# Seven instead of five layer-1 weight blocks resident beside a recurrent scan

## The chip, the cores and the metric

One core of one Trainium2 chip runs the whole program. The metric is the device time of one execution in microseconds (us); less is better. Engines are named as in the profile: PE (TensorE matmuls), PEld (its weight loads), DVE (VectorE), ACT (ScalarE), POOL (GpSimd) and SP (SyncE, which issues all DMAs here).

## The reference

A recurrence over 768 time steps (4 batches, 8 heads, head size 40, a 40x40 state each) gives a tensor that is read as 3072 tokens of 320 features. Two gated feed-forward layers follow, both 320 to 1536 to 320:

```python
for t in range(S):
    y[:, :, t] = einsum('bhd,bhde->bhe', r[t], state)
    Sa = einsum('bhde,bhe->bhd', state, a[t])
    state = state * w[t] - einsum('bhd,bhe->bhde', Sa, b[t]) + einsum('bhd,bhe->bhde', v[t], k[t])
x = y.transpose(0, 2, 1, 3).reshape(3072, 320)
x = (silu(x @ w_gate) * (x @ w_val)) @ w_out        # layer 1
x = (sigmoid(x @ w_gate2) * (x @ w_val2)) @ w_out2  # layer 2
```

## The kernel before, in words

**The recurrence.** `attention` cuts the 768 steps into 12 chunks of 64 and turns each chunk into matmuls. For chunk m, `prep_a` forms the products of keys and queries (`kps`, L364, in four groups, with ACT L372 and DVE L374 behind each), and leaves a matrix `bn`. `prep_b` sends a part of `bn` through DRAM (L393 and L400) and then solves a triangular system on DVE: L409, L410 and 15 pairs of L417 (multiply) and L423 (reduce), each pair longer than the last. In this text that is **the solve** of chunk m, and a **step** is the time from one solve's L409 to the next one's. `chain` carries the state through the chunk (L506, L524, L535), and `post` forms the chunk's output `ysb` (L570 to L607).

**The feed-forward.** The tokens come in 12 blocks of 256 (one for each chunk), and each layer's weights in 12 blocks of 128 hidden features. One token block with one weight block is a **unit**: `gate` (16 matmuls of 128x256, L809; ACT L813 and L817; DVE L815 and L816; POOL L818) and `add` (6 matmuls of 128x320, L827). Each layer has 144 units. Weights come as float64 bit patterns, and `load_w` turns them into a high and a low part. It does a block in three **pieces**, each with one DMA (L699), five DVE instructions (L707, L711, L712, L716, L717), one on ACT (L727) and three or four on POOL (L708, L729 to L735).

**What runs beside what.** While the recurrence runs, layer-1 units run between its matmuls. This is `extra(m, ys)`: it splits chunk m's output into high and low parts (`split`, L755 to L771; **the split** in this text), stores the split block to DRAM (`xd`), and runs a unit with each weight block that is in SBUF by then. The number is kept in `used`. Five blocks are loaded early: three into a pool `wa` before the first chunk's units, two into `wt` and `wq`, which hold decay powers before that. Seven more (`more`) go into tiles of the recurrence as these come free, from chunk 10 on. After the recurrence, `stream` runs the units that are left of layer 1 (`w1[used[blk]:]`, with `load_x`, `each1` and `end1`) and then all of layer 2. `load_w2` converts the 12 weight blocks of layer 2 beside the rest of layer 1, one piece in each of three units of a token block.

**What sets the order.** `merge` (L624) interleaves the generators of an iteration m: `cp(m)`, `prep_b(m + 1)`, `prep_a(m + 2)`, `ahead(m)` (which holds `extra(m - 1)`) and `more`. Each stream has a pair (width of a step, offset), such as `NX = (0.1658, 0.2)` for `ahead`, and the least offset plus steps times width goes next. A scheduler then orders each engine's instructions. The engines run them strictly in that order.

Of the kernel before, what the change touches and what calls it, by code (L numbers as in the profile page):

```python
# [18 lines left out]
P = 128  # L19
# [1 line left out]
W = 16  # L21
C = 64
NS = 16
NFA = 5
NWB = 2
DM = H * D
PW = 64 + D
DFF = 1536
# [11 lines left out]
F_HIGH = (1.875 - 2.0**-23) * 2.0**16  # L40


def attention(ctx, tc, st, ident, ins, banks, extra, more):

# [507 lines left out]
    def post(m):  # L554
# [4 lines left out]
        for bp in range(2):  # L559
# [26 lines left out]
            for part in range(2):  # L586
                for h in range(H):
                    hp, h2 = divmod(h, 2)
                    for b2 in range(2):
# [11 lines left out]
                            stop=part == 1 and h == H - 1,  # L601
                            tile_position=(0, 64 * b2),
                        )
            ysb = wk.tile([P, DM + 64], F32, tag="ysb", name="ysb", bufs=3)
            yf, pf = yps.rearrange("p h d -> p (h d)"), pn[:, DM * bp : DM * bp + DM]
            nc.vector.tensor_tensor(out=ysb[:, 0:DM], in0=yf, in1=pf, op=ALU.mult)
            nc.vector.tensor_tensor(out=ysb[:, DM:], in0=yf[:, 256:DM], in1=pf[:, 256:DM], op=ALU.mult)  # L607
# [54 lines left out]
    for m in range(-1, NCH + 1):  # L662
        todo = []
        if 0 <= m < NCH:
            todo.append((cp(m), *NP))
        if 0 <= m < NCH - 1:
            todo.append((prep_b(m + 1), *(NB if m else QC)))
        if 2 <= m + 2 < NCH:
            todo.append((prep_a(m + 2), *(NA if m else QD)))
        todo.append((ahead(m), *(NX if m > 0 else QX)))  # L670
        if more is not None:

            free = {NCH - 2: [f"lq{NCH % 3}", f"tkb{NCH % 3}"]}
            free[NCH - 1] = [f"lq{(NCH + 1) % 3}", f"tkb{(NCH + 1) % 3}", "part0"]
            free[NCH] = ["part1", f"lq{(NCH + 2) % 3}", "part3", f"tkb{(NCH + 2) % 3}", "ut", "rbd", "part2"]
            todo.append((more(free.get(m, []), (raw_of(wk, ("sn", "zt", "x1t")), (pmm, "mm")) if m >= NCH - 1 else None), *NM))
        merge(todo)
# [308 lines left out]
def rwkv_moe_kernel(ctx, tc, r, k, v, w, a, b, aw0, aw, aa, akb, av, avt, art, w1a, w2a, out):  # L986
# [11 lines left out]
    with ExitStack() as c1:  # L998
# [1 line left out]
        x_p, h_p = pool("m_x", 1), pool("m_h", 2)  # L1000
        wa, st = pool("m_wa", NFA - 2), pool("at_static", 1)
        w1, w2, tags, spare_tags, used = [], [], [], [], []
        first = [(wa, "w8")] * (NFA - 2) + [(st, "wt"), (st, "wq")]

        with ExitStack() as c2:
            pool2 = lambda n, b: c2.enter_context(tc.tile_pool(name=n, bufs=b, space=PSUM))
            ffn = None

            def banks():

                nonlocal ffn
                ptp, pzy, pqu, pg, pmm, po = (pool2(f"a_{n}", 1 + (n == "tp")) for n in ("tp", "zy", "qu", "pg", "mm", "po"))
                ffn = Ffn(nc, ident, ([raw_of(st)], x_p, h_p, ptp, [(pg, "gv")], po), True)
                return ptp, pzy, pqu, pmm, po

            def more(new, spare):
                if spare is not None and len(ffn.raw) == 1:
                    ffn.raw.append(spare[0])
                    ffn.pg.append(spare[1])
                n = NF - len(w1)  # L1020
                spare_tags.extend(new[n:])
                for tag in new[:n]:
                    tags.append(tag)
                    yield from ffn.load_w(st, tag, layers[0], len(w1))
                    w1.append(ffn.w)

            def extra(m, ys):
                if m >= 0:
                    used.append(len(w1))
                    x = ffn.split(ys.pop(m))  # L1030
                    nc.sync.dma_start(out=xd[m], in_=x.bitcast(F32))
                    yield
                    yield from ffn.ffn(x, w1[: used[m]], True, "po")
                    for u in range(2):
                        ob = h_p.tile([P, DM], F32, tag="ob", name="ob", bufs=1)
                        nc.scalar.copy(out=ob, in_=ffn.o[u])
                        nc.sync.dma_start(out=xs[1][2 * m + u], in_=ob)
                        yield
                for f in {-2: range(NFA - 2), 1: range(NFA - 2, NFA)}.get(m, ()):
                    yield from ffn.load_w(*first[f], layers[0], f)  # L1040
                    w1.append(ffn.w)

            attention(c2, tc, st, ident, (aw0, aw, aa, akb, av, avt, art), banks, extra, more)

        with ExitStack() as c2:
            pool2 = lambda n, b, **kw: c2.enter_context(tc.tile_pool(name=n, bufs=b, **kw))
# [14 lines left out]

            ahead = load_w2()

            def load_x(blk):
                ffn.x = (x_q, x_p)[blk % 2]
                x = ffn.new_x()
                nc.sync.dma_start(out=x.bitcast(F32), in_=xd[blk])
                yield x

            def split_x(blk):  # L1070
                xin = y_p.tile([P, 2, DM + 64], F32, tag="xin", name="xin")
                src = xs[1][2 * blk : 2 * blk + 2].rearrange("u p e -> p u e")
                nc.sync.dma_start(out=xin[:, :, 0:DM], in_=src)
                nc.sync.dma_start(out=xin[:, :, DM:], in_=src[:, :, 256:DM])
                yield
                ffn.x = (x_q, x_p)[blk % 2]
                yield from ffn.split_steps([xin[:, 0], xin[:, 1]])

            parts = {}
# [1 line left out]
            def each1(blk, f):  # L1081
# [2 lines left out]
                    nc.sync.dma_start(out=part, in_=xs[1][2 * blk : 2 * blk + 2].rearrange("u p e -> p u e"))  # L1084
                if 1 <= f <= 3:
                    next(ahead, None)
                if blk == NB - 1 and f == NF - 1 - used[blk]:
                    for _ in ahead:
                        pass

# [38 lines left out]
                flag.append(fl)  # L1129

            flag, jobs, seen = [], [], []
            for blk in range(NB):
                jobs.append((w1[used[blk] :], True, "po", load_x(blk), partial(each1, blk), partial(end1, blk)))
            for blk in range(NB):
                jobs.append((w2, False, "po", split_x(blk), partial(check, blk), partial(end2, blk)))
# [54 lines left out]
```

## Time and profile before

| | |
|---|---|
| three runs, us | 1457.96, 1460.96, 1463.65 (median 1460.96) |
| the profiled execution, span, us | 1462.6 |
| PE, DVE, POOL, ACT busy, us | 1282.7, 858.1, 678.0, 535.1 |
| mean granted TensorE clock | 0.890 |

The span runs from the first instruction to the last of the one profiled execution; no other time is listed for that execution, and its span lies 1.6 us above the median of the runs. A busy PE is not a PE at its peak, since the ends of matmuls are modelled and overlap. The granted clock is given as a share of full speed: 1.0 is 2.4 GHz and 0.5 is 1.2 GHz. The profile counts an fp32 matmul of the recurrence twice (two passes), so four `kps` matmuls of the program are eight in a row of the trace.

### The profile page before, as it was taken

Reading aid. Unit: us, or ns where it says so; the run is one execution under the profiler, and the core shown is the slowest. Engines: PE = TensorE matmul, PEld = TensorE weight load, DVE = VectorE, ACT = ScalarE, POOL = GpSimd, SP = SyncE. Lnnn points to the kernel's source line nnn. Section 1 sums busy time; section 2 is a strip of 40 time slices with the busy share of each in tenths; the row PEclk is TensorE's granted clock in tenths of the full one; section 3 lists DMA queues with packets and bytes.
Section 4 is the critical chain, followed back from the end, with each engine's and each line's share of the span. In section 5 each row is a group of like instructions: output and inputs, shape, how many; then the busy total and the mean of one; then the engine's idle time right before and its main releaser. Section 6 shows DMA issues by size and latency. Waiting matters only on the chain.

```text
span 1462.6 us, 32637 instructions
## 1 busy us (share of the span) xinstructions
PE 1282.7 (88%) x13197; PEld 1207.8 (83%) x13197; DVE 858.1 (59%) x1644; ACT 535.1 (37%) x1260; POOL 678.0 (46%) x800
## 2 busy tenths in 40 slices
PE   4548867789899899887979999999999999999996
PEld 4447756678888888786979988889999999999996
DVE  8679759388756865876687999886311122112111
ACT  5223524253445444533433332333333333333331
POOL 4378468352213222245587888996222222222221
PEclk7556858696989999886999999999999999999998
DMA  5854884946355446425234654442100000100000
GB/s 139 206 114 107 170 195 94 187 97 159 88 125 140 102 119 147 93 62 132 87 99 155 185 164 132 140 135 95 63 21 21 21 21 22 30 21 21 12 13 17
DMA packets 242096, 144.49 MB, mean 99 GB/s; under 512 B 186768, under 2 KB 218512, under 8 KB 241552
## 3 DMA queue, kind: packets, MB, share of 16 engines
q1 hardware_dynamic: 241936, 142.31, 37.6%
q8 instruction: 106, 1.74, 0.5%
q14 instruction: 54, 0.44, 0.1%
HBM read 104.00 MB, written 38.27 MB: 97 GB/s over the span
## 4 chain that ended last, share of the span: by engine, by line
PE 43%; DVE 30%; DMA 10%; POOL 5%; SPq 5%; issue 5%; ACT 1%; POOLq 0%; DVEq 0%; ACTq 0%
PE g L809 21%; PE po L827 11%; DVE pr L417 7%; PE gv L809 4%; DVE part L423 4%; DMA sn<-nd 3%; DVE dt L712 3%; DVE dt L711 2%; POOL dt L708 2%; SPq L219 2%; DVE ds L717 2%; DMA raw<-in_w_dram 2%; DVE g L815 1%; PE kps L364 1%; DVE dt L707 1%
## 5 line engine op out<-in xcount | busy, mean ns | idle before, releaser
L809 PE MATMUL g<-x,w 128*128 128x256 f32 x3552 | 495.3, 284 | 12.8 <-DVE g L815 11.8
L809 PEld LDWEIGHTS g<-x,w 128*128 128x128 f32 x3552 | 462.8, 190 | 19.0 <-DVE g L815 16.7
L818 POOL TENSOR_TENSOR hl<-g,hh 128x256 fp32r<-128x256 f32 x288 | 220.5, 768 | 452.8 <-ACT hh L817 409.5
L816 DVE TENSOR_TENSOR g<-g,g 128x256 f32<-128x256 f32 x222 | 93.7, 422 | 307.7 <-PE g L809 297.7
L827 PE MATMUL po<-w,hh 128*128 128x320 f32 x1152 | 230.0, 314 | 2.8 <-ACT hh L817 1.4
L817 ACT CAST hh<-g 128x256 fp32r<-128x256 f32 x288 | 117.0, 406 | 302.8 <-DVE g L816 276.4
L809 PE MATMUL gv<-x,w 128*128 128x256 f32 x1056 | 173.4, 318 | 30.4 <-DVE g L816 18.2
L809 PEld LDWEIGHTS gv<-x,w 128*128 128x128 f32 x1056 | 152.9, 217 | 38.2 <-DVE g L816 24.2
L827 PEld LDWEIGHTS po<-w,hh 128*128 128x128 f32 x1152 | 179.0, 191 | 4.6 <-ACT hh L817 2.6
L417 DVE TENSOR_TENSOR pr<-part,sn 128x4 f32<-128x4 f32 (+4 forms) x180 | 150.1, 834 | 4.0
L827 PE MATMUL po<-w,hl 128*128 128x320 f32 x576 | 145.1, 318 | 2.9 <-POOL hl L818 2.9
L813 ACT ACTIVATE g<-g 128x256 f32<-128x256 f32 x222 | 85.1, 384 | 142.5 <-PE g L809 109.4
L708 POOL TENSOR_SCALAR dt<-dt 128x384 f32<-128x384 f32 (+1 forms) x72 | 109.2, 1519 | 40.9 <-DVE dt L707 38.0
L729 POOL TENSOR_TENSOR dt<-dt,w 128x384 f32<-128x384 f32 (+1 forms) x72 | 79.3, 1101 | 78.4 <-ACT w L727 32.3
L827 PEld LDWEIGHTS po<-w,hl 128*128 128x128 f32 x576 | 93.8, 191 | 5.2 <-POOL hl L818 4.2
L423 DVE TENSOR_REDUCE part<-pr 128x2 f32<-128x4 f32 (+4 forms) x180 | 88.9, 494 | 4.0
L364 PE MATMUL kps<-lq,kbt 104*128 104x128 f32 x384 | 69.4, 338 | 18.6 <-DVE lq L374 15.6
L364 PEld LDWEIGHTS kps<-lq,kbt 104*128 104x128 f32 x384 | 61.8, 244 | 23.2 <-issue 13.2
L727 ACT CAST w<-dt 128x384 fp32r<-128x384 f32 (+1 forms) x72 | 35.6, 495 | 98.6 <-DVE dt L712 91.5
L570 PE MATMUL aps<-rbd,ut 104*128 104x128 f32 x384 | 61.5, 307 | 9.3 <-DVE ysb L607 3.0
L707 DVE TENSOR_SCALAR dt<-raw 128x384 int32<-128x384 int32 (+1 forms) x72 | 44.9, 624 | 40.2 <-DMA raw<-in_w_dram 34.1
L372 ACT ACTIVATE bn<-kps 64x256 f32<-64x256 f32 x96 | 36.4, 379 | 84.5 <-PE kps L364 46.6
(129 smaller groups left out, 1762.1 us busy)
## 6 DMA issues: line engine op xcount, KB each, us to landing
raw<-in_w_dram SPq DMA_DIRECT2D x48, 384.0 KB
xd<-x SPq DMA_DIRECT2D x12, 896.0 KB
x<-xd SPq DMA_DIRECT2D x12, 896.0 KB
raw<-in_w_dram SPq DMA_DIRECT2D x24, 320.0 KB
pn<-pd SPq DMA_DIRECT2D x46, 160.0 KB
ld<-in_a_kb_dram SPq DMA_DIRECT2D x22, 320.0 KB
ld<-rd SPq DMA_DIRECT2D x44, 160.0 KB
sn<-nd SPq DMA_DIRECT2D x24, 256.0 KB
```

The costliest lines, as they stand in the source:

```text
L364: nc.tensor.matmul(kps[:, n].rearrange("p h t -> p (h t)"), lhsT=kbt[0:PW, n, :], rhs=lq[m % 3][0:PW, 4 * g4 + n].rearrange("p h t -> p (h ...
L417: nc.vector.tensor_tensor(out=o, in0=xs[:, 0:kk, None, 0:n].to_broadcast([P, kk, 2, n]), in1=sn[:, None, 0:n, n : n + 2].rearrange("p o s ...
L423: nc.vector.tensor_reduce(out=xs[:, 0:kk, n : n + 2], in_=o, axis=AX.X, op=ALU.add)
L570: nc.tensor.matmul(aps[:, n, h2], lhsT=ut[0:PW, x, 2 * h2 : 2 * h2 + 2].rearrange("p u s -> p (u s)"), rhs=rbd[0:PW, x, h2].rearrange("p b ...
L708: nc.gpsimd.tensor_scalar(out=t.bitcast(F32), in0=t.bitcast(F32), scalar1=F_LOW, scalar2=F_HIGH, op0=ALU.max, op1=ALU.min)
L729: sub(out=tf, in0=tf, in1=w.bitcast(F32), op=ALU.subtract)
L809: nc.tensor.matmul(gv[n], lhsT=p, rhs=q, start=e == 0, stop=e == len(seq) - 1)
L813: nc.scalar.activation(out=g, in_=gv[0], func=AF.Sigmoid)
L816: nc.vector.tensor_tensor(out=g, in0=gv[1], in1=g, op=ALU.mult)
L817: nc.scalar.copy(out=hh, in_=g)
L818: self.heng.tensor_tensor(out=hl, in0=g, in1=hh.bitcast(F32), op=ALU.subtract)
L827: self.nc.tensor.matmul(ops[u], lhsT=p[:, us], rhs=q, start=first and n == 0, stop=last and n == 2)
```

## The change

The tables that set sizes and pools:

```diff
-NFA = 5
-NWB = 2
+NFA = 7
+NWB = 1
@@ post
-            ysb = wk.tile([P, DM + 64], F32, tag="ysb", name="ysb", bufs=3)
+            ysb = wk.tile([P, DM + 64], F32, tag="ysb", name="ysb", bufs=2)
@@ merge loop of attention
-        todo.append((ahead(m), *(NX if m > 0 else QX)))
+        todo.append((ahead(m), *((1.33 / (6 + units(m - 1)), NX[1]) if m > 0 else QX)))
@@ rwkv_moe_kernel
-        first = [(wa, "w8")] * (NFA - 2) + [(st, "wt"), (st, "wq")]
+        first = [(wa, "w8")] * 3 + [(st, "wt"), (st, "wq")] + [(wa, "w8")] * (NFA - 5)
@@ extra
-                for f in {-2: range(NFA - 2), 1: range(NFA - 2, NFA)}.get(m, ()):
+                for f in {-2: range(3), 1: range(3, 5), 2: range(5, 6), 3: range(6, NFA)}.get(m, ()):
                     yield from ffn.load_w(*first[f], layers[0], f)
@@ call of attention: units is
+ lambda m: min(len(w1), NFA) + (3 if m == 1 else 0)
@@ kernel
-    nc = _bacc.Bacc("TRN2", target_bir_lowering=False, num_devices=1)
+    nc = _bacc.Bacc("TRN2", target_bir_lowering=False, num_devices=1, dynamic_dma_scratch_size=512)
```

The pool `wa` has five tiles instead of three. Weight blocks 5 and 6 are loaded behind the units of token blocks 2 and 3, before iterations in which no weights were loaded; so `more` has two blocks less to load for layer 1, and layer 2 finds two more tiles free. The space comes from the scratch for dynamic transfers, one of three `ysb` buffers and one of two `wb` buffers. The width of `ahead`'s step now follows the number of units. The numbers in `used` go from 3, 3, 5, 5, 5, 5, 5, 5, 5, 6, 8, 11 to 3, 3, 5, 6, 7, 7, 7, 7, 7, 8, 10, 12, so 82 units of layer 1 instead of 66 run beside the recurrence, and 62 instead of 78 behind it. The last token block has all 12 units there and gets no job in `stream`:

```diff
-            for blk in range(NB):
+            left = [blk for blk in range(NB) if used[blk] < NF]
+            for blk in left:
                 jobs.append((w1[used[blk] :], True, "po", load_x(blk), partial(each1, blk), partial(end1, blk)))
```

`load_x` and `split_x` take their two buffers in turn of use instead of by the block's parity, and the pieces of `load_w2` that are left are taken in the last block of `left`.

Three places show what this does to the order. The first is on PE, in a step in the middle of the recurrence (chunks 7 to 10 are alike), between the first and the second `kps` group behind the split. `gv` is the sum of a unit's gate matmuls, the number behind `w_` is that of a weight block, `po` is `add`, `sps` and `qps` belong to `chain`, and `tp` are transposes. Before:

```order
L364 MATMUL kps<-lq_206,kbt 128x128 x4
L535 MATMUL sps<-part_203,tkb_91 40x40 x5
L809 MATMUL gv<-x,w_633 128x256 x12
L304 MATMUL tp<-ident,part_86 104x128 x4
L304 MATMUL tp<-ident,tkb_90 104x128 x4
L364 MATMUL kps<-lq_206,kbt 128x128 x4
```

Now:

```order
L364 MATMUL kps<-lq_206,kbt 128x128 x4
L304 MATMUL tp<-ident,part_86 104x128 x4
L809 MATMUL gv<-x,w_675 128x256 x16
L304 MATMUL tp<-ident,tkb_90 104x128 x4
L827 MATMUL po_6390<-w_633,hh 128x320 x2
L827 MATMUL po_6391<-w_633,hh 128x320 x2
L304 MATMUL tp<-ident,part_86 104x128 x4
L506 MATMUL qps<-part_203,lq_207 64x40 x4
L827 MATMUL po_6390<-w_633,hl 128x320
L827 MATMUL po_6391<-w_633,hl 128x320
L506 MATMUL qps<-part_203,lq_207 64x40 x3
L364 MATMUL kps<-lq_206,kbt 128x128 x4
```

The first unit (w_633) now stands ahead of the first of these two groups, and the second unit's 16 gate matmuls and the first unit's `add` stand between them. Between the second and the third group there is one unit as before, so one unit more stands ahead of the third.

The second is on ACT at the end of the solve in the same step. `xt` is the copy that waits for the solve's last L423, `x` is the split, `kbt` and `bn` belong to `prep_a`, `qs` and `part` to `chain`. Before:

```order
L519 COPY qs<-qps 128x320
L372 ACTIVATE bn<-kps 64x256
L360 COPY kbt<-tp 104x512
L761 CAST x<-xtp 128x512
L372 ACTIVATE bn<-kps 64x256
L528 COPY part_203<-ups 64x320 x2
L529 COPY part_86<-ups 128x4x2x40
L765 CAST x<-xtp 64x256
L766 CAST x<-xtp 64x256
L427 COPY xt<-part_88 128x512
```

Now:

```order
L519 COPY qs<-qps 128x320
L372 ACTIVATE bn<-kps 64x256
L427 COPY xt<-part_88 128x512
L372 ACTIVATE bn<-kps 64x256
L761 CAST x<-xtp 128x512
L765 CAST x<-xtp 64x256
L766 CAST x<-xtp 64x256
L528 COPY part_203<-ups 64x320 x2
```

The split stood ahead of the copy `xt`, and now stands behind it.

The third is on DVE in the solve of chunk 6, which had no weight conversion in it (`am` and `ysb` belong to `post`). Now:

```order
L417 TENSOR_TENSOR pr<-part_88,sn 128x14x14
L578 TENSOR_TENSOR am<-aps,part_86 128x512
L711 TENSOR_SCALAR dt<-dt 128x320
L423 TENSOR_REDUCE part_88<-pr 128x7x2
L712 SCALAR_TENSOR_TENSOR dt<-raw,dt 128x320
L417 TENSOR_TENSOR pr<-part_88,sn 128x16x16
L716 TENSOR_SCALAR ds<-dt 128x320
L423 TENSOR_REDUCE part_88<-pr 128x8x2
L717 SCALAR_TENSOR_TENSOR ds<-raw,ds 128x320
```

Pieces of weight block 6 stand between the pairs of the solve. The solves of chunks 4 to 6 and what follows each have 3, 4 and 3 pieces now, and had 2, 2 and none.

## Rows read from the trace of the kernel before

**Rows 1.** The page: the span, and the gate matmuls beside the recurrence.
```profile
span 1462.6 us, 32637 instructions
...
L809 PE MATMUL gv<-x,w 128*128 128x256 f32 x1056 | 173.4, 318 | 30.4 <-DVE g L816 18.2
```
**Rows 2.** Busy time by stretch (start:end, length, each engine, clock, DMA, GB/s).
```profile
288.00:431.00 143.00, 125.25 (x1640) 113.71 (x1637) 106.84 (x204) 62.47 (x144) 46.20 (x50) 0.84 0.53 129
431.00:637.00 206.00, 188.25 (x2725) 170.16 (x2723) 142.13 (x269) 97.12 (x222) 55.91 (x68) 0.92 0.47 113
637.00:764.00 127.00, 106.50 (x1434) 95.77 (x1429) 94.98 (x182) 43.87 (x102) 75.65 (x87) 0.87 0.33 90
764.00:1006.00 242.00, 224.97 (x1690) 216.51 (x1689) 213.87 (x422) 77.59 (x197) 206.70 (x222) 0.99 0.47 151
1040.00:1449.00 409.00, 409.00 (x3237) 408.97 (x3236) 80.81 (x184) 134.01 (x343) 112.92 (x166) 1.00 0.07 20
```
**Rows 3.** The same for DVE L816 alone: one for each unit.
```profile
288.00:431.00 143.00, 5.48 (x13) 0.84 0.53 129
431.00:637.00 206.00, 8.46 (x20) 0.92 0.47 113
637.00:764.00 127.00, 6.70 (x16) 0.87 0.33 90
```
**Rows 4.** The same for DVE L717 alone: one for each piece.
```profile
288.00:431.00 143.00, 2.14 (x4) 0.84 0.53 129
764.00:1006.00 242.00, 33.56 (x40) 0.99 0.47 151
```
**Rows 5.** DVE in order of time (start, us): first and last of two solves.
```profile
326.30 1.21 DVE L409 TENSOR_TENSOR nt<-sn 128x512 f32<-128x512 f32 x1 [2.95 <-DMA sn<-nd]
...
360.45 1.07 DVE L423 TENSOR_REDUCE part<-pr 128x30 f32<-128x900 f32 x1
...
483.07 1.13 DVE L409 TENSOR_TENSOR nt<-sn 128x512 f32<-128x512 f32 x1 [2.64 <-DMA sn<-nd]
...
508.07 1.09 DVE L423 TENSOR_REDUCE part<-pr 128x30 f32<-128x900 f32 x1
```
**Rows 6.** PE in order of time behind the split of that step.
```profile
518.34 2.17 PE L809 MATMUL gv<-x,w 128*128 128x256 f32 x16
520.34 0.75 PE L827 MATMUL po<-w,hh 128*128 128x320 f32 x4
...
521.26 0.56 PE L827 MATMUL po<-w,hl 128*128 128x320 f32 x2
...
522.59 1.06 PE L364 MATMUL kps<-lq,kbt 104*128 104x128 f32 x8
```
**Rows 7.** DVE in order of time, from there to the next solve.
```profile
515.40 0.43 DVE L815 TENSOR_TENSOR g<-gv,g 128x256 f32<-128x256 f32 x1 [0.54 <-ACT g L813]
...
529.84 0.99 DVE L545 TENSOR_TENSOR part<-sps,part 40x320 f32<-40x320 f32 x2 [0.52 <-PE sps L535]
532.49 1.13 DVE L409 TENSOR_TENSOR nt<-sn 128x512 f32<-128x512 f32 x1 [1.66 <-DMA sn<-nd]
```
**Rows 8.** ACT in order of time around the end of that solve.
```profile
506.60 0.59 ACT L761 CAST x<-xtp 128x512 fp32r<-128x512 f32 x1 [2.05 <-PE xtp L755]
...
508.07 0.38 ACT L372 ACTIVATE bn<-kps 64x256 f32<-64x256 f32 x1
509.20 1.13 ACT L427 COPY xt<-part 128x512 f32<-128x512 f32 x1 [0.74 <-DVE part L423]
```
**Rows 9.** DVE and POOL in order of time: one L417 shape in two solves.
```profile
297.18 0.73 DVE L417 TENSOR_TENSOR pr<-part,sn 128x324 f32<-128x324 f32 x1
...
298.60 1.49 POOL L708 TENSOR_SCALAR dt<-dt 128x384 f32<-128x384 f32 x1 [4.89 <-DVE dt L707]
...
441.39 1.13 DVE L417 TENSOR_TENSOR pr<-part,sn 128x324 f32<-128x324 f32 x1
...
441.07 2.20 POOL L326 TENSOR_TENSOR tkb<-ld 128x320 f32<-128x320 f32 x2
```

More of the change, by code (lines that the diff above doesn't have):

```diff
@@ L40, with attention @@
 F_HIGH = (1.875 - 2.0**-23) * 2.0**16
-def attention(ctx, tc, st, ident, ins, banks, extra, more):
+def attention(ctx, tc, st, ident, ins, banks, extra, more, units):
     nc = tc.nc
@@ L1038, in extra @@
                         yield
-                for f in {-2: range(NFA - 2), 1: range(NFA - 2, NFA)}.get(m, ()):
+                for f in {-2: range(3), 1: range(3, 5), 2: range(5, 6), 3: range(6, NFA)}.get(m, ()):
                     yield from ffn.load_w(*first[f], layers[0], f)
                     w1.append(ffn.w)
-            attention(c2, tc, st, ident, (aw0, aw, aa, akb, av, avt, art), banks, extra, more)
+            attention(c2, tc, st, ident, (aw0, aw, aa, akb, av, avt, art), banks, extra, more, lambda m: min(len(w1), NFA) + (3 if m == 1 else 0))
         with ExitStack() as c2:
@@ L1062, in rwkv_moe_kernel, with next_x @@
             ahead = load_w2()
+            turns = [0]
+            def next_x():
+                ffn.x = (x_q, x_p)[turns[0] % 2]
+                turns[0] += 1
             def load_x(blk):
-                ffn.x = (x_q, x_p)[blk % 2]
+                next_x()
                 x = ffn.new_x()
@@ L1075, in split_x @@
                 yield
-                ffn.x = (x_q, x_p)[blk % 2]
+                next_x()
                 yield from ffn.split_steps([xin[:, 0], xin[:, 1]])
@@ L1086, in each1 @@
                     next(ahead, None)
-                if blk == NB - 1 and f == NF - 1 - used[blk]:
+                if blk == left[-1] and f == NF - 1 - used[blk]:
                     for _ in ahead:
```

## The prediction

> **What bounds the kernel now.** I read the busy times by stretch first [rows 2], then DVE's counts of units and of weight pieces in the same stretches [rows 3, 4], and then one step of the recurrence instruction by instruction [rows 5 to 8]. The reader is to see three kinds of time.
>
> In the last 409 us only layer 2 runs, and PE is busy for all of it at the full clock (1.0 granted, the 2.4 GHz level) [rows 2]. That gives the price of a unit that nothing hides: 409 / 144 = 2.84 us.
>
> In the four steps from 431 to 637 us PE is busy for 188.25 of 206 us at a granted clock of 0.92 [rows 2], with 20 units in them [rows 3]. So a step takes 51.5 us, holds 5 units, and leaves PE idle for only 4.4 us. What sets a step is a ring: DVE's solve (483.07 to 509.16, 26.1 us) [rows 5], then the split and the `kps` groups on PE, the last of which ends at 523.65 [rows 6], then the way of `bn` through DRAM, until the next L409 at 532.49 [rows 7]. PE's work between the solve's end and the last `kps` lies on the ring. PE's work elsewhere lies beside DVE's.
>
> From 764 to 1006 us no engine has room: PE 224.97, DVE 213.87 and POOL 206.70 of 242 us [rows 2], with 40 weight pieces [rows 4]. Beside the recurrence 1056 / 16 = 66 units run in all [rows 1].
>
> **What the change moves.** 16 units move from behind the recurrence to beside it: by the order 2 into the steps from 288 to 431 us, 8 into the four steps from 431 to 637, 5 into the stretch up to the last token block, and 1 into that block. Six pieces (two weight blocks) move from the last block's stretch into the steps from 288 to 431. The sum is made against the profiled execution, 1462.6 us [rows 1], 1.6 us above the median of the runs.
>
> *Four middle steps, 7 units instead of 5.* On the ring, one unit more stands ahead of the third `kps` group. By its rows it takes 2.00 us to the next instruction, 0.75 and 0.56 [rows 6], with overlaps some 3.0 us. The split now stands behind the copy `xt`, which waits for the solve's end. Its first cast began at 506.60, well ahead of that end; now it comes behind a copy of 1.13 and an L372 of 0.38 and takes 0.59 itself [rows 8], so the gates begin some 2.1 us later. In the solve, DVE has one unit more (0.43 + 0.42), and the pair L545, which stood in the wait for the DMA (0.99, ended before 532.49) [rows 7], now stands behind L409. That is 3.0 + 2.1 + 0.85 + 0.99 = 6.9 us for a step. The other bound: two units are 5.7 us of PE, and PE's 4.4 us of idle time could hide most of it, which leaves 1.3. I take 5.0, nearer to the ring, since the idle time lies in the solve and the DMA wait while the added unit lies ahead of both. Four steps: **+20** (ends +5 and +28).
>
> *288 to 431 us: 2 units and 6 pieces more* (13 units and 4 pieces before) [rows 3, 4]. The solve of chunk 5, with two pieces in it, took 326.30 to 361.52, 35.2 us, against 26.1 for one with none [rows 5]: 4.5 us for a piece. All six in solves would be 27, and half a unit of DVE with them 28. DVE is idle for 143 - 106.84 = 36 us of the stretch [rows 2], which could hide everything. By the order about half of the added pieces stand inside solves: 3 x 4.5 and a little for the units, **+15** (ends 0 and +28).
>
> *637 to 764 us: 5 units more.* All paid, they are 5 x 2.84 = 14 us. PE is idle for 127 - 106.5 = 20.5 us here, and the clock is at 0.87 [rows 2], so they could also be free. In the middle: **+8** (ends 0 and +14).
>
> *764 us to the end of layer 1* (276 us: 11 units of the last block and 78 behind it, so 89 units at 3.10; now 12 + 62 = 74). In proportion, 15 units fewer are 46.5 us. Against this stand the pieces: 40 in 242 us are 6.05 us each [rows 2, 4]. If they set the pace, 36 take 218 us, then some ten units follow at 2.6 (what 276 - 242 = 34 us for 13 units gives), 244 us in all, only 32 less. All three engines are near full here, so I stay near the proportion: **-43** (ends -32 and -47).
>
> *Edits at nothing.* Layer 2 keeps its 144 units and its order of jobs. The two-deep `ysb` is read by the split, early in the next step, long before the next chunk's `post` writes; if that split came late, `post` would wait for it, and the ring with it. One `wb` tile less is covered by two more freed tiles; without them, layer 2's first pieces would wait for the last layer-1 units. All DMAs are issued by SP, none by POOL, so I give the smaller scratch no price. SP gets the raw loads of the six pieces earlier; each waits in SP's queue for the piece before it, and `bn`'s way through DRAM stands behind it. That is part of the 4.5 us for a piece.
>
> Sum: 20 + 15 + 8 - 43 = **0**. The profiled execution would stay at 1462.6, and the median at 1461.0. The units cost beside the recurrence what they cost behind it.
>
> **A rule against the change.** In the solve of chunk 7 the 324-element L417 took 1.13 us, with a POOL instruction from 441.07 on beside it; in the solve of chunk 4, where POOL was idle for 4.89 us until 298.60, the same shape took 0.73 [rows 9]. So a clash costs at least 0.4 us, and each unit and each piece brings POOL work into a solve. The Trainium skill (SBUF — State Buffer, "SBUF: two separate sides") says why: DVE with two SBUF inputs and GpSimd share a pair of ports under an exclusive lock, and the loser waits for the whole instruction. By this rule the added units and pieces cost more than their own DVE time; the sum would be that of the second rival, not 0.
>
> **Rivals.** *Faster: PE's holes take the units.* The granted clock of 0.84 to 0.92 between 288 and 637 us [rows 2] says that PE falls to 1.2 GHz after idle stretches, and more work in these would keep it at 2.4. Then the steps pay the lower ends: +5 in the middle, +5 and +3 around them, -45 behind, together -32: 1429. For it speaks that 206 us hold 17.75 of idle PE time; against it, that the idle time is not where the third `kps` group waits. It decides if a middle step stays under 53.5 us.
>
> *Slower: DVE and POOL shut each other out.* The place is the solve. One clash of 0.4 us more in each middle step makes 7.3 x 4 = 29, the pieces stretch three solves by 28, the stretch up to the last block costs its +8, and behind it units and pieces are no thinner than before, so that the pieces hold it to -36. Together +29: 1490. It decides if a middle step takes over 57 us. For it speak the rows of the 1.13 us L417; against it, that its sum needs nearly every upper end at once.
>
> *The change doing less than it says* I leave out: the order has 82 units of layer 1 ahead of `stream`.
>
> **How the numbers follow.** What a measurement of this kernel can tell from no change is about 0.5%, 7.3 us: 1453.7 to 1468.3. No change, 1461.0, is the likeliest: 0.40. The first rival, and what else ends under 1453.7, has 0.33, the second and what ends over 1468.3 has 0.27; the lower ends are each a little easier to reach, as a scheduler that fills holes is at work in every term. The ends of the terms add up to -42 and +38. Not all lie at one side, and the range takes some three quarters of it each way and so reaches to the two rivals: 1431 to 1486. The forecast's own range is 1450 to 1472.
>
> **What would show it.** The L409 of chunks 7 to 11 stand 56.5 us apart (51.5 before): the first term. Solves 4 to 6 last some 13 us longer together: the second. The last unit of layer 1 ends some 43 us sooner after the last block's split: the fourth. 82 x 16 `gv` matmuls, and layer 2 at 409 us: nothing else changed. The prediction is wrong if a middle step stays near 52 us, or if the last stretch shrinks by under 32 us.

## The result and the profile after

| | us | ratio to before, 95% interval |
|---|---|---|
| before, in the same comparison | 1457.7 (1453.8 to 1464.5, 20 runs) | |
| the change | 1466.7 (1461.9 to 1472.9, 20 runs) | 1.0061 [1.0047, 1.0075] |
| profiled spans | 1462.6 and 1468.2 | +5.6 us |

The forecast was no change at 1461.0, the median of three runs. The time lies in its own range of 1450 to 1472, and within its 1453.7 to 1468.3 for "no change"; but the 20 runs of the kernel before have a median 3.3 us lower than those three, and as a ratio the change is slower by 0.6%, a little more than the 0.5% that the prediction called no change. The sum of 0 came out as +5.6 us in the two profiles. Stretch by stretch, with the prediction's terms (a unit is taken here from the end of its L816 on DVE):

| stretch | before | after | measured | term (ends) |
|---|---|---|---|---|
| start to the solve of chunk 4 | 287.9 | 284.2 | -3.7 | none |
| solves 4 to 7 | 143.3 | 156.4 | +13.1 | +15 (0, 28) |
| solves 7 to 11 | 205.4 | 230.1 | +24.7 | +20 (5, 28) |
| solve 11 to the first unit of the last block | 132.5 | 136.8 | +4.3 | +8 (0, 14) |
| from there to the end of layer 1 | 271.1 | 237.5 | -33.6 | -43 (-32, -47) |
| layer 2 | 409.0 | 409.1 | 0 | 0 |

Every stretch here and below comes from one profiled execution of a kernel. How far a stretch can be trusted is seen where two kernels have the same order on every engine up to the last solve. E7 and E10 (below) have the change's order, and their solves 4 to 7 took 152.6 and 155.1 us against 156.4, their solves 7 to 11 227.5 and 227.6 against 230.1; E6 has that of the kernel before, and took 142.1 and 202.9 against 143.3 and 205.4. So a difference of less than some 4 us in one stretch tells nothing.

The page after, its span and the gate matmuls beside the recurrence (1312 / 16 = 82 units):

```profile
span 1468.2 us, 32545 instructions
...
L809 PE MATMUL gv<-x,w 128*128 128x256 f32 x1312 | 202.3, 308 | 34.2 <-DVE g L816 24.1
```

Busy time by stretch after, with columns as in [rows 2]:

```profile
284.00:441.00 157.00, 139.51 (x1645) 126.40 (x1645) 122.77 (x236) 65.73 (x152) 74.80 (x74) 0.79 0.52 129
441.00:671.00 230.00, 216.00 (x2839) 195.90 (x2840) 147.15 (x285) 102.52 (x238) 61.91 (x76) 0.90 0.41 101
671.00:803.00 132.00, 118.78 (x1635) 107.22 (x1630) 95.90 (x188) 46.79 (x109) 76.26 (x86) 0.96 0.31 87
803.00:1020.00 217.00, 196.22 (x1440) 188.22 (x1439) 191.03 (x372) 65.25 (x171) 178.66 (x194) 0.98 0.47 156
1045.00:1454.00 409.00, 409.00 (x3234) 408.97 (x3233) 80.00 (x181) 133.62 (x343) 112.47 (x165) 1.00 0.07 20
```

The units (DVE L816) in the first three of these stretches, as [rows 3]:

```profile
284.00:441.00 157.00, 6.26 (x15) 0.79 0.52 129
441.00:671.00 230.00, 11.81 (x28) 0.90 0.41 101
671.00:803.00 132.00, 8.84 (x21) 0.96 0.31 87
```

And the weight pieces (DVE L717), as [rows 4]:

```profile
284.00:441.00 157.00, 6.49 (x10) 0.79 0.52 129
...
803.00:1020.00 217.00, 34.51 (x35) 0.98 0.47 156
```

The units and pieces went where the order put them: 15, 28 and 21 units against 13, 20 and 16 [rows 3], and 10 pieces against 4 in the first stretch [rows 4]. In the middle stretch PE is busy for 28 us more than before for 8 units, and is idle for 14 of 230 us instead of 17.75 of 206 [rows 2]: its holes took almost nothing. Nor did the clock gain there: 0.79 and 0.90 against 0.84 and 0.92; it rose in the third stretch alone, 0.96 against 0.87. One step of the middle after, as [rows 5] (first and last of a solve, and the next L409):

```profile
496.63 1.13 DVE L409 TENSOR_TENSOR nt<-sn 128x512 f32<-128x512 f32 x1 [2.54 <-DMA sn<-nd]
...
523.40 1.08 DVE L423 TENSOR_REDUCE part<-pr 128x30 f32<-128x900 f32 x1
...
554.77 1.13 DVE L409 TENSOR_TENSOR nt<-sn 128x512 f32<-128x512 f32 x1 [2.38 <-DMA sn<-nd]
```

The step is 58.1 us long, the solve 27.9. The four middle steps take 56.0, 58.1, 59.7 and 56.2, 57.5 in the mean; 56.5 was predicted.

### The profile page after: what moved, and what is told of

Its sections match the earlier page's. It is cut to its first block, busy times and chain, and to the rows that moved or that the text cites. A ratio compares the mean times of both kernels' runs of the same rounds, so it can differ in the third digit from the quotient of the medians.

```text
span 1468.2 us, 32545 instructions
## 1 busy us (share of the span) xinstructions
PE 1288.6 (88%) x13197; PEld 1212.2 (83%) x13197; DVE 855.7 (58%) x1642; ACT 532.3 (36%) x1260; POOL 682.1 (46%) x800
## 4 chain that ended last, share of the span: by engine, by line
PE 45%; DVE 29%; DMA 11%; issue 5%; POOL 4%; SPq 3%; ACT 2%; DVEq 0%; POOLq 0%; ACTq 0%
PE g L809 20%; PE po L827 11%; DVE pr L417 7%; PE gv L809 4%; DVE part L423 3%; DMA sn<-nd 3%; DVE dt L711 2%; DVE dt L712 2%; POOL dt L708 2%; DMA raw<-in_w_dram 2%; DVE g L815 2%; PE yps L596 2%; PE tp L304 2%; PE kps L364 2%; DVE g L816 2%
## 5 line engine op out<-in xcount | busy, mean ns | idle before, releaser
L809 PE MATMUL g<-x,w 128*128 128x256 f32 x3296 | 463.0, 284 | 6.1 <-DVE g L815 5.7
L809 PEld LDWEIGHTS g<-x,w 128*128 128x128 f32 x3296 | 432.7, 191 | 9.1 <-DVE g L815 8.3
L818 POOL TENSOR_TENSOR hl<-g,hh 128x256 fp32r<-128x256 f32 x288 | 228.1, 793 | 446.8 <-ACT hh L817 419.9
L816 DVE TENSOR_TENSOR g<-g,g 128x256 f32<-128x256 f32 x206 | 87.1, 423 | 306.2 <-PE g L809 301.4
L809 PE MATMUL gv<-x,w 128*128 128x256 f32 x1312 | 202.3, 308 | 34.2 <-DVE g L816 24.1
L809 PEld LDWEIGHTS gv<-x,w 128*128 128x128 f32 x1312 | 181.2, 209 | 41.5 <-DVE g L816 30.6
L417 DVE TENSOR_TENSOR pr<-part,sn 128x4 f32<-128x4 f32 (+4 forms) x180 | 150.7, 837 | 3.8
L813 ACT ACTIVATE g<-g 128x256 f32<-128x256 f32 x206 | 78.6, 384 | 118.0 <-PE g L809 106.0
L423 DVE TENSOR_REDUCE part<-pr 128x2 f32<-128x4 f32 (+4 forms) x180 | 88.7, 493 | 3.5
L374 DVE TENSOR_TENSOR lq<-kps,part 64x256 f32<-64x256 f32 x96 | 40.5, 422 | 41.4 <-ACT bn L372 39.5
```

The lines of the kernel that those rows point to most:

```text
L417: nc.vector.tensor_tensor(out=o, in0=xs[:, 0:kk, None, 0:n].to_broadcast([P, kk, 2, n]), in1=sn[:, None, 0:n, n : n + 2].rearrange("p o s ...
L423: nc.vector.tensor_reduce(out=xs[:, 0:kk, n : n + 2], in_=o, axis=AX.X, op=ALU.add)
L809: nc.tensor.matmul(gv[n], lhsT=p, rhs=q, start=e == 0, stop=e == len(seq) - 1)
L813: nc.scalar.activation(out=g, in_=gv[0], func=AF.Sigmoid)
L816: nc.vector.tensor_tensor(out=g, in0=gv[1], in1=g, op=ALU.mult)
L818: self.heng.tensor_tensor(out=hl, in0=g, in1=hh.bitcast(F32), op=ALU.subtract)
```

## The experiments

Twelve kernels ran, each beside the kernel before. Ratios are to it, with 95% intervals. "Profile" times are those of the profiled execution.

**E1: the copy `xt` off ACT.** The first term had 2.1 us for a middle step from the split's wait behind this copy. Here the copy moves to POOL. In the four middle steps PE's order stays as in the change; ahead of them the edit changed the order on every engine, and solves 4 to 7 took 170.6 us against 156.4. So the whole time of E1 doesn't test the copy, and the middle steps do.

```diff
-nc.scalar.copy(out=xt, in_=xs.rearrange("p r t -> p t r"))
+nc.gpsimd.tensor_copy(out=xt, in_=xs.rearrange("p r t -> p t r"))
```

> The change, with one instruction moved: the copy xt (L427) that waits for the solve's end goes from ACT to POOL, so the split no longer stands behind it. PE's order stays word for word. Ring theory (what stands between the solve's end and the last kps sets a step): the split begins some 2 us sooner, steps 7 to 10 fall from 57.5 us to about 55.5, and the whole from 1466.7 to about 1458. Rival (the solve itself grows, by DVE's and POOL's clashes): the copy reads SBUF on POOL now, so the step stays at 57.5 or grows, and the whole stays at 1466 or over.

Measured: 1470.9 us, ratio 1.0089 [1.0056, 1.0123]. The middle steps took 55.4, 58.1, 59.8 and 55.6, in the mean 57.2 against 57.5. The 2.1 us for a step were not there. DVE and ACT in order of time at the end of the solve of chunk 8 in E1:

```profile
530.65 1.08 DVE L423 TENSOR_REDUCE part<-pr 128x30 f32<-128x900 f32 x1
```

```profile
534.56 0.59 ACT L761 CAST x<-xtp 128x512 fp32r<-128x512 f32 x1 [1.23 <-PE xtp L755]
```

The copy no longer stands ahead of the split on ACT, and the split still begins 2.8 us after the solve's end, because PE has not yet run its transposes `xtp` (L755). PE is behind when the solve ends. In the change, where the solve of chunk 8 ends at 524.48, it was 2.8 us as well, so the copy was not what held the split:

```profile
527.30 0.59 ACT L761 CAST x<-xtp 128x512 fp32r<-128x512 f32 x1 [0.73 <-PE xtp L755]
```

**E2: the old width of the units' stream.** The change with one line undone:

```diff
-        todo.append((ahead(m), *((1.33 / (6 + units(m - 1)), NX[1]) if m > 0 else QX)))
+        todo.append((ahead(m), *(NX if m > 0 else QX)))
```

> The change with the old width for a step of the units' stream (0.1658), and still 7 resident blocks and 82 units. In the order one unit less stands ahead of the third kps group behind the split, and the split stands ahead of one kps group less. Ring theory: steps 7 to 10 lose some 3 us, 57.5 to about 54.5, the whole some 10 us: 1456. Rival (7 units cost what they cost wherever they stand, on PE, DVE and POOL): steps stay at 57 to 58, the whole at 1466.

Measured: 1448.1 us (1443.5 to 1455.3), ratio 0.9942 [0.9917, 0.9968]. Both forecasts missed: the step (55.75, below) lies between them, and the whole is shorter than either said. It is faster than both kernels: the seven resident blocks, with the smaller pools that make room for them, are worth 0.6%, and the new width takes back twice that. Busy time by stretch in E2:

```profile
288.00:440.00 152.00, 131.41 (x1651) 119.75 (x1650) 122.67 (x236) 65.33 (x152) 70.04 (x73) 0.82 0.53 136
440.00:663.00 223.00, 208.08 (x2839) 190.87 (x2838) 145.02 (x283) 103.08 (x238) 59.47 (x75) 0.91 0.42 104
663.00:788.00 125.00, 117.22 (x1630) 107.71 (x1629) 93.01 (x188) 46.37 (x109) 77.65 (x86) 0.96 0.32 89
788.00:1000.00 212.00, 194.51 (x1448) 185.00 (x1448) 187.46 (x375) 66.86 (x174) 181.36 (x195) 1.00 0.50 160
```

The same 8 units more are in the four middle steps, which now take 223 us: 20 us of PE for 8 units, and 55.75 us for a step. PE's idle time is 15 us, about as before, and a unit added to a step costs 2.2 us. The change needs 8 us more of busy PE for the same work. DVE and ACT at the end of the solve of chunk 8 in E2:

```profile
521.13 1.12 DVE L423 TENSOR_REDUCE part<-pr 128x30 f32<-128x900 f32 x1
```

```profile
529.13 0.58 ACT L761 CAST x<-xtp 128x512 fp32r<-128x512 f32 x1
```

The split begins 6.9 us behind the solve's end, later than the 2.8 us of the change, and the step is shorter. So the time from the solve's end to the split, which the prediction's ring counts in full, doesn't set the step.

**E3: units later in the step.** The change with the offset of the units' stream at 0.5 instead of 0.2.

```diff
-        todo.append((ahead(m), *((1.33 / (6 + units(m - 1)), NX[1]) if m > 0 else QX)))
+        todo.append((ahead(m), *((1.33 / (6 + units(m - 1)), 0.5) if m > 0 else QX)))
```

> The change with an offset of 0.5 instead of 0.2 for the units' stream: 7 units in a step, but in the order only 7 gate matmuls of a unit stand between the split and the last kps group. Ring theory: steps 7 to 10 fall to what PE's work leaves, about 53 us, and the whole to about 1450. Rival (the units cost the same wherever they stand): 57 to 58 us and 1466. A third way: the units pile up behind the last kps group and the solve's end comes to wait for them; then steps stay over 56 us with longer solves.

Measured: 1470.7 us, ratio 1.01 [1.0061, 1.0138]; middle steps of 56.0, 59.1, 59.4 and 53.7, in the mean 57.0. With all units later the steps stay as long, as the rival said; the solves were no longer than in the change (25.7 to 28.5 us), so the third way isn't seen. But the length is made up otherwise. The four steps, columns as in [rows 2]:

```profile
446.20:674.40 228.20, 203.59 (x2801) 182.41 (x2800) 146.93 (x281) 99.69 (x233) 62.18 (x77) 0.96 0.41 100
```

PE is busy for 12 us less than in the change, at a clock of 0.96, and idle for 24.6 us instead of 14. So neither PE's busy time nor the clock alone sets a middle step; what PE waits for in E3 stays open.

**E4: six blocks.** The change with one number:

```diff
-NFA = 7
+NFA = 6
```

> Six resident blocks instead of seven, 75 units beside the recurrence. In the order the stretch from the split to the last kps group holds as many units as with seven, one unit less stands in the solve. Ring theory: steps 7 to 10 stay at 56 to 57.5 us, and the tail is longer by some 7 units, so the whole is no better than with seven: 1466 to 1475. Rival (each unit costs its share): steps lie half way, 54.5 us, and the whole half way, 1462.

Measured: 1472.3 us, ratio 1.0107 [1.007, 1.0144]. The middle steps took 53.7 us with six units, between 51.35 (five) and 57.5 (seven), even under the 54.5 of the rival; the whole is where the ring theory had it, so neither forecast holds in both. With the formula's width throughout (five units in E5, below) the three lengths are 52.8, 53.7 and 57.5: a unit costs something each time, but not the same. Solves 4 to 7 took 156.2 us, as much as with seven blocks (156.4) although three pieces fewer are in them. So the +13 there isn't a price of pieces alone, as the prediction's second term had it.

**E5: the new width alone.** The kernel before with the change's width formula and five blocks (the argument `units` is passed as in the change):

```diff
-        todo.append((ahead(m), *(NX if m > 0 else QX)))
+        todo.append((ahead(m), *((1.33 / (6 + units(m - 1)), NX[1]) if m > 0 else QX)))
```

> The kernel before with the change's formula for the width of the units' stream (1.33 over 6 plus the number of units: 0.121 for five units in place of 0.1658) and nothing else; five blocks, 66 units. E2 differs from the change in this width alone and is 1.5% shorter. Theory A, the formula costs by itself, whatever the number of units: slower than before by 8 to 18 us, ratio 1.005 to 1.012, middle steps 52.5 to 54 us instead of 51.4, and some us more from the last solve to the end of layer 1. Theory B, the formula only costs with seven units in a step, since it spreads the units over places that fit five but not seven: within 4 us of before (ratio 0.997 to 1.003), middle steps 51 to 52 us. Theory C, the formula serves five units as it serves nothing else: faster, ratio under 0.997.

Measured: 1480.9 us (1476.8 to 1484.2), ratio 1.0145 [1.0124, 1.0166]; theory A, and more than its upper end; the middle steps took 52.8 us. With E2 this makes a table of two by two, ratios to before:

| | old width | formula |
|---|---|---|
| five blocks | 1 | 1.0145 (E5) |
| seven blocks | 0.9942 (E2) | 1.0061 (the change) |

The product of the two single effects is 1.0086, near the 1.0061 of both. By stretch (profiles, us against before):

| stretch | two blocks (E2) | formula (E5) | both |
|---|---|---|---|
| to the solve of chunk 4 | -0.3 | -1.8 | -3.7 |
| solves 4 to 7 | +9.1 | +5.1 | +13.1 |
| solves 7 to 11 | +17.6 | +5.6 | +24.7 |
| solve 11 to the end of layer 1 | -42.7 | +8.5 | -29.2 |

Where the formula costs is seen in part. Of the 5.6 us that it costs from solve 7 to solve 11 in E5, 5.0 lie in the first step, from 434.5 us, which took 56.8 us where the kernel before took 51.9, with the same five units in it. First DVE in order of time inside E5's solve:

```profile
449.58 0.69 DVE L578 TENSOR_TENSOR am<-aps,part 128x512 f32<-128x512 f32 x1 [1.56 <-PE aps L570]
...
455.02 0.69 DVE L578 TENSOR_TENSOR am<-aps,part 128x512 f32<-128x512 f32 x1 [1.93 <-PE aps L570]
```

DVE runs in order, so these waits for `post`'s matmuls stand in the middle of the solve, which takes 33.1 us instead of 26.7. PE in order of time in that step of E5:

```profile
437.75 0.86 PE L827 MATMUL po<-w,hh 128*128 128x320 f32 x4 [2.36 <-ACT hh L817]
...
439.80 1.94 PE L596 MATMUL yps<-part,rbd 104*64 104x40 f32 x32
441.52 1.92 PE L596 MATMUL yps<-tkb,am 128*64 128x40 f32 x32
...
447.46 2.08 PE L570 MATMUL aps<-rbd,ut 104*128 104x128 f32 x8
...
452.90 2.08 PE L570 MATMUL aps<-rbd,ut 104*128 104x128 f32 x8
```

The same place before:

```profile
434.30 3.60 PE L809 MATMUL gv<-x,w 128*128 128x256 f32 x16 [2.21 <-DVE g L816]
...
438.27 1.13 PE L596 MATMUL yps<-part,rbd 104*64 104x40 f32 x32
439.23 1.11 PE L596 MATMUL yps<-tkb,am 128*64 128x40 f32 x32
...
443.73 1.16 PE L570 MATMUL aps<-rbd,ut 104*128 104x128 f32 x8
```

The narrower width had moved the unit whose gate matmuls stood here (434.30 before) ahead of the solve. None stand on PE from 434.5 to 458 us, and the recurrence's own matmuls run at 1.2 GHz: 1.94 and 2.08 us where the kernel before needs 1.13 and 1.16. The stretches in E5 and in the kernel before, columns as in [rows 2]:

```profile
434.50:458.00 23.50, 21.14 (x302) 18.79 (x300) 18.04 (x38) 8.81 (x19) 3.66 (x5) 0.64 0.23 67
```

```profile
431.20:455.00 23.80, 20.96 (x370) 18.38 (x368) 22.53 (x43) 9.96 (x21) 8.53 (x10) 0.93 0.25 66
```

PE is as busy in both (21.1 and 21.0 us) at a granted clock of 0.64 and 0.93. But the missing gate matmuls alone don't explain it: E5's next step has the same order in that place, and its first 23.5 us are

```profile
491.40:514.90 23.50, 17.81 (x392) 15.69 (x387) 22.61 (x44) 10.43 (x22) 5.54 (x7) 1.00 0.30 86
```

at the full clock, with more matmuls done in less busy time. That step took 50.2 us, and the two behind it 52.2 and 51.8. One thing differs ahead of the slow stretch: PE was idle for 2.36 us there (437.75 above), and for 0.81 us in the next step. In the kernel before PE was idle as long at that place (2.21 us) and the gate matmuls followed. Whether it takes both, an idle PE and no gate matmuls behind it, no run here shows.

Over the whole run DVE's wait for `aps` (sum in us, times, longest) in the list of waits goes up by 13.6 us with the formula at five blocks and by 5.1 at seven, and by 3.6 with the blocks. Before:

```profile
DVE am L578 <- PE aps L570: 10.6, 10, 3.0
```

The change:

```profile
DVE am L578 <- PE aps L570: 19.3, 17, 2.3
```

E2:

```profile
DVE am L578 <- PE aps L570: 14.2, 12, 2.9
```

E5:

```profile
DVE am L578 <- PE aps L570: 24.2, 17, 2.7
```

This wait goes with the width but isn't its price: E3, with the formula's width and the later offset, has 11.4 us of it and is no faster than the change.

**E6 and E7: layer 2's weight conversion cut to copies**, in the kernel before and in the change, by the same edit in `load_w`:

```diff
+            if layer[1] is False:
+                ts(out=t, in0=hi, scalar1=0x7FFFFFFF, scalar2=None, op0=ALU.bitwise_and)
+                nc.scalar.copy(out=wh[:, at : at + sz], in_=t.bitcast(F32))
...
+                yield
+                continue
```

> The kernel before, in which the conversion of layer 2's weights is cut to copies: a piece has one DVE instruction and two ACT copies and nothing on POOL, and the rest of the conversion is left out, so layer 2 computes with other weights. To be read with E7, the same cut in the change. Pacing theory, the weight pieces set the pace from the last solve to layer 1's last unit: without them this stretch falls from 403.6 to some 360 us or less (units alone, 94 of them behind the last solve at about 2.84 us make 267, and chain and post of the last chunk come on top of it), and E7's stretch is shorter than this one's by 40 us or more, since only the number of units is left to count (16 fewer at 2.5 to 2.84). Rival, PE itself sets this stretch: it falls by under 15 us, and the difference between E7 and this one stays the 29 us that it was between the change and the kernel before (403.6 and 374.3).

> The change with the same cut as E6. Pacing theory: from the last solve to layer 1's last unit some 320 us or less (374.3 in the change), and 40 us or more under E6; the whole run 8 to 16 us faster against E6 than the change is against the kernel before, so E7 ends below E6. Rival (PE sets the stretch): over 360 us, 29 us under E6, and the whole run stays about 9 us above E6, as the change stays above the kernel before.

Measured: E6 1442.4 us, 0.9886 [0.9868, 0.9904]; E7 1437.2 us, 0.9867 [0.9843, 0.9892]. E7 is below E6 by 5 us where the change is 9 us above the kernel before; the intervals of E6 and E7 overlap, so which of them is faster is open, but that the 9 us are gone is clear of noise. From the last solve to the end of layer 1 E6 took 385.8 and E7 345.1, 40.7 apart, against 29.2. Both lengths are above the 360 and 320 that the pacing theory gave, so the pieces don't pace the stretch; they add to it. The rival failed as well: E6's stretch fell by 17.8 us, not by under 15, and the difference is not 29. From the last block's split on, in the order before, E6:

```profile
763.00:1040.00 277.00, 259.52 (x1959) 251.05 (x1960) 228.61 (x455) 89.54 (x228) 218.86 (x240) 0.99 0.44 143
```

```profile
759.00:1018.00 259.00, 252.12 (x1958) 250.12 (x1959) 127.45 (x312) 106.19 (x289) 82.42 (x108) 0.99 0.46 153
```

and in the order the change, E7:

```profile
803.00:1045.00 242.00, 220.77 (x1630) 212.51 (x1630) 203.10 (x400) 73.68 (x193) 188.41 (x208) 0.98 0.45 149
```

```profile
795.00:1011.00 216.00, 210.48 (x1632) 208.70 (x1633) 101.95 (x260) 91.90 (x254) 55.59 (x77) 0.99 0.50 167
```

Without the conversions PE is idle for 5.5 to 7 us and the stretch shrinks by 259 - 216 = 43 us for 15 units, 2.87 us a unit, near the 2.84 us that a unit of layer 2 takes with nothing hidden. Four pieces of layer 1 are left whole in E6's stretch and none in E7's, so some of the 43 us are theirs. With the conversions PE is idle for 17.5 us before and 21 after. What the cut takes away, 36 pieces of layer 2 before and 35 after, costs 277 - 259 = 18 us before and 242 - 216 = 26 after. The 8 us between them have two readings that E6 and E7 don't part, since they differ in the width as well: the same pieces beside fewer units are hidden less, or the formula's order costs here too. E2, with the change's units and pieces and the old width, speaks for the second:

```profile
788.00:1024.00 236.00, 218.51 (x1636) 209.00 (x1636) 198.86 (x401) 74.86 (x196) 190.12 (x209) 1.00 0.48 153
```

It is 6 us shorter than the change here and 41 us shorter than the kernel before, with PE idle for 17.5 us as before.

**E8 and E12: other widths**, in the change, a constant in place of the formula (0.102 for seven units): 0.22 and 0.14.

```diff
-        todo.append((ahead(m), *((1.33 / (6 + units(m - 1)), NX[1]) if m > 0 else QX)))
+        todo.append((ahead(m), *((0.22, NX[1]) if m > 0 else QX)))
```

> The change with the width 0.22 for the units' stream, in place of the formula's 0.102 for seven units; E2 had 0.1658 and 1448.1 us. If a wider step is better throughout (units come later against the recurrence's own work, which is then never kept waiting): 1435 to 1446 us. If 0.1658 is near the best (units that come too late are left over for the end of an iteration and the next split waits for them): 1450 to 1470 us, with middle steps of 57 us and more again. E3 moved all units later by an offset and gained nothing, which speaks for the second.

> The change with the width 0.14 throughout, between the formula's 0.102 (1466.7 us) and E2's 0.1658 (1448.1); 0.22 (E8) gave 1448.5. If the cost grows steadily as the width shrinks below 0.166: about 1453 to 1460 us. If it is a matter of single units that happen to stand well or badly in the order, no such dose is seen: anything from 1445 to 1470 us, 1448 or less included.

Measured: E8 1448.5 us, 0.992 [0.9902, 0.9938], between its two forecasts, with middle steps of 55.0 us and not 57; E12 1457.6 us, 1.0005 [0.9985, 1.0024], as a steady cost said. In the whole time the dose is steady: 1466.7 at the formula (0.102 from iteration 5 on), 1457.6 at 0.14, 1448.1 at 0.1658, and then flat, 1448.5 at 0.22. By stretch it is not: from the formula to 0.14 the start of the last solve stays (670.7 and 672.3 us) and all of the gain lies behind it (374.3 and 364.5). E8 has the middle steps a little shorter than E2 (220.0 us for four) and the stretch behind the last solve longer (364.8 against 360.8).

**E9, E10 and E11: the width by iteration.** The old width in iterations 1 to 9 alone (E9), in the last three alone (E10), and 0.22 early with 0.1658 late (E11).

```diff
-        todo.append((ahead(m), *((1.33 / (6 + units(m - 1)), NX[1]) if m > 0 else QX)))
+        todo.append((ahead(m), *(QX if m <= 0 else NX if m <= 9 else (1.33 / (6 + units(m - 1)), NX[1]))))
```

> The change with the old width 0.1658 in iterations 1 to 9 and the formula in the last three (10 to 12). In the profiles, E2 (old width everywhere) was 21 us shorter than the change: 8 us of it lay ahead of the last solve and 13 us behind it. If the formula costs by placing units badly among the recurrence's own matmuls wherever it stands, the costs add: this kernel saves the first part, the last solve starts at 662 to 666 (670.7 in the change, 663.1 in E2) and the time from it to the end of layer 1 stays near 374; 1456 to 1462 us in all. Rival: the stretch behind the last solve is only longer because of the state in which the earlier iterations leave the engines; then this kernel is as good as E2, 1446 to 1451 us.

> The mirror of E9: the formula in iterations 1 to 9, the old width 0.1658 in the last three. If the costs add: the last solve starts at 668 to 672, as in the change, and the stretch from it to the end of layer 1 falls to some 361; 1452 to 1457 us. Rival (the state left by the earlier iterations): the stretch stays at some 374 and the kernel at 1463 to 1468 us.

> Seven blocks with the width 0.22 in iterations 1 to 9 and 0.1658 in the last three: the best stretches of E8 (last solve at 659.0) and of E2 (360.8 behind it). If the stretches add, 659 + 361 and some 423 us of the rest make 1443 in the profile, and the runs 1441 to 1446 us, the best of the study. If a width only moves work from one stretch to the next (E8 and E2 end within 0.4 us of each other), no better than E2: 1447 to 1451 us.

Measured: E9 1458.2 us, 1.0009 [0.9991, 1.0026]; E10 1461.7 us, 1.0026 [1.0009, 1.0043]; E11 1454.1 us, 0.9965 [0.9948, 0.9982]. In E9 the last solve started at 662.6 and the rest of layer 1 took 375.1, as the adding theory said. In E10 it started at 668.5 and the rest took 369.2, between the two forecasts, as the whole time is. So the formula costs in both parts: against E2, 13.6 us in the early iterations alone (E10), 10.1 in the last three alone (E9) and 18.5 in both, somewhat less than the sum. E11 missed both forecasts: its last solve started at 658.8, as in E8, but the rest took 373.0, longer than in either parent. E2 and E11 have the same width in the last iterations and E11 needs 12 us more there, so what a width costs in them depends on what the ones ahead leave behind; by what, these runs don't settle. E2 and E8 stay the best of the kernels that compute the whole result, level with each other.

## Why the prediction was right and where not

**The stretches were near, the reason for the middle steps was not shown.** The first term priced a ring: one unit ahead of the third `kps` group (3.0 us), the split behind the copy (2.1), DVE's own (1.84). E1 took the second away and the step stayed; E3 moved units later and the steps stayed; in E2 the split came later still and the step was shorter. With the old width PE's work grew by 5 us a step and its idle time shrank by 0.7, so two units cost 4.4 (E2), where the ring had 6.9 and full hiding 1.3. The remaining 1.8 of the measured 6.2 came with the formula. So "nearer to the ring", 5.0, was near by luck: the waits that it added up are not the ones that the steps show. What does set a step stays open: PE's idle time in it is 3.2 to 4.4 us in the kernel before, the change, E1 and E2, but 6.2 in E3 and 6.1 in E5.

**The step that failed is the one left out: the width.** The formula stood in the change, and the prediction gave it no term of its own: it read the order that the formula makes, and priced parts of it (the unit ahead of the third `kps` group, the split behind the copy) as if the blocks had brought them. E5 prices the width at 1.45%, some 21 us, and E2's reversal at 18.5 us: the largest single effect of the change, and the sign of the result. The forecast absorbed it in terms that were set high for other reasons: +20 and +15 against E2's +17.6 and +9.1, and -35 for the last two stretches against -42.7. That errors of both signs added up to a time within its range is luck. How the width costs is shown in single places only, and in full by none of the runs.

**The second term** (+13.1 for 15) was right in size. Its reading, 4.5 us a piece, is not borne out by E4: three pieces fewer, the same time; E2 and E5 split it into 9.1 for the blocks and 5.1 for the formula. The prediction let all six pieces come from the last stretch and then reckoned there with 36 of 40, four fewer; the rows show 35, five fewer.

**The fourth term** was mis-sized: -33.6 for -43, near the end of -32 that the pieces gave, and the third with +4.3 for +8 gave part of it back. E2, with the old width, has -40.7 in the same place, so the blocks gave nearly what the proportion said, and the width took 7 us back. The other bound's cause, the pieces, is real as a cost (E6 and E7: 18 and 26 us) but doesn't pace the stretch; whether fewer units hide less of it is not shown.

**Rivals.** The first, PE's holes take the units and the clock gains, fell: the granted clock went down in the first two stretches, and PE's idle time in the middle shrank by some 3 us in E2 for 8 units. E2 beats both kernels in spite of that, by what the moved units save behind the recurrence. The second's mark, a middle step over 57 us, was passed (57.5; 56.9 in E7 and E10, which repeat this order), but not by its mechanism, a lock between DVE and POOL. All L417 of the four middle steps (DVE busy) before and after:

```profile
431.20:636.60 205.40, 47.56 (x60) 0.92 0.47 113
```

```profile
440.60:670.70 230.10, 46.52 (x60) 0.90 0.41 101
```

They took 1 us less in sum, with 8 more units and their POOL work beside them. The Trainium skill (SBUF — State Buffer, "SBUF: two separate sides") states an exclusive lock between a DVE instruction with two SBUF inputs and a GpSimd instruction that reads SBUF. The longer times moved between shapes here, the 324-element L417 from 1.13 to 0.76 us and the 16-element one from 0.19 to 0.36, and did not grow in sum.

**Edits at nothing.** Layer 2 took 409.1 us in place of 409.0. The smaller scratch, the two-deep `ysb` and the single `wb` were not tried apart; E2 carries all three and is faster than the kernel before.

## What to carry to other kernels

When a change brings a planner's number along with the real edit, price that number as a part of its own: here the two blocks gained 0.6% and the retuned width lost twice as much. A step's length that comes out near is no proof of the ring that it was added up from: take one wait of the ring away, as E1 did, and see whether the step moves. And when one stretch of a trace shows a striking cause, look at the next repetition of the same order before calling it the cause: E5's slow step had three fast ones behind it.

## What had not been expected of the hardware

PE can be busy and still be at 1.2 GHz. The change's four middle steps and a part of the second, columns as in [rows 2]:

```profile
440.60:496.60 56.00, 50.74 (x711) 45.96 (x709) 36.53 (x70) 25.35 (x59) 15.68 (x18) 0.97 0.44 111
496.60:554.80 58.20, 56.28 (x719) 51.17 (x715) 36.17 (x71) 25.51 (x59) 14.23 (x18) 0.85 0.42 106
554.80:614.50 59.70, 57.95 (x745) 52.80 (x739) 36.20 (x71) 25.51 (x59) 14.24 (x18) 0.86 0.42 104
614.50:670.70 56.20, 51.13 (x679) 46.08 (x677) 38.34 (x75) 26.15 (x61) 17.47 (x22) 0.94 0.34 81
...
511.00:529.00 18.00, 17.36 (x217) 15.28 (x216) 14.26 (x18) 9.78 (x21) 5.50 (x6) 0.62 0.52 127
```

PE runs the same order in all four, but for the end of the last. The two with less idle time have the lower clock and are 2 to 3.7 us longer. In the part of the second, PE is busy for 17.4 of 18 us, nearly all with the recurrence's matmuls of 32 to 128 columns (a unit adds two of its last ones and four of the next unit's gate), and the clock is 0.62. The prediction held that PE falls to 1.2 GHz after idle stretches, and the Trainium skill (TensorE: Matmul & The Clock Gate, "Part 1: The HAM clock gate (the "warmup" mystery)") ties the gate to how busy PE has been; here the granted clock was down in a stretch that the profile shows as busy, as in E5. The same instructions in the step ahead of it ran at the full clock:

```profile
455.00:470.00 15.00, 11.37 (x213) 9.77 (x213) 13.63 (x16) 8.52 (x17) 5.55 (x5) 1.00 0.50 136
```

In E10, which has the same order again, the four steps took 56.4, 56.2, 58.3 and 56.6 us. So neither the order nor PE's busy time settles which step gets the lower clock; what does, no run here shows.
